# Joint attention and feed-forward on one core: last chunk's scores in quarters, a range check by bits and sums, last sums of x kept in SBUF, shape changes counted in the planner

## The chip, the cores and the metric

The kernel runs on one core of a Trainium2 chip. The time is the device time of one execution in microseconds. Five engines work side by side, each through its own queue in order: TensorE (PE in the profile, its weight loads PEld), VectorE (DVE), ScalarE (ACT), GpSimd (POOL) and SyncE (SP), which here issues every DMA.

## What is computed

Four batches of 12 heads, 448 positions, 64 values a head, everything in float32; then a feed-forward layer from 768 to 2048 and back.

```python
scores = scale * np.matmul(q, k.transpose(0, 1, 3, 2))     # q, k, v: (4, 12, 448, 64)
scores = cap * np.tanh(scores / cap)
scores = scores - np.max(scores, axis=-1, keepdims=True)
attn = np.exp(scores)
attn = attn / (np.sum(attn, axis=-1, keepdims=True) + 1e-09)
x = np.matmul(attn, v)             # then heads side by side: (1792, 768)
h = x @ w_in                       # w_in (768, 2048)
g = np.where(h >= 1, h, np.where(h <= -1, 0.0, (h + 1) ** 2 / 4.0))
out = (g @ w_out).astype(np.float32)
```

## The kernel before

**Numbers.** A float32 factor is split into a high and a low f16 half, and a product is three f16 matmuls (high by high, high by low, low by high). The weights arrive as 64-bit floats, read as pairs of 32-bit words, and are converted by bit operations (`piece`, L288 to L295, with a copy of the float32 in DRAM, zd). That fits weights in a bounded range only, so a second pass, `piece_check` (L305, L307), loads each of the 56 half pieces again into one of two buffers z0, z1 (32 halves of w_in with 384 elements a partition, 24 of w_out with 512) and takes their largest and smallest magnitude by two VectorE reductions. `piece_done` and `verdict` (L325 to L337) bring this and checks on x, g and the exponentials to one flag, with a reduction over the partitions on GpSimd (L330); at the end the flag is loaded (L1385) and a branch (L1386) skips a general program if all is in range.

**Attention.** Heads go in pairs n = 0 to 23, six to a batch. The 448 keys of a pair are chunks c = 0 to 3: three of 128 keys for each head, with two blocks of scores each, and a last one that holds the last 64 keys of both heads, with zeros in between. `qk` (L381) makes a chunk's scores in PSUM by three matmuls per block; for c < 3 they use 64 rows (L381, 64\*128) and the two heads' matmuls run in two halves of the array; for c = 3 they are full (128\*128). `expo` (L389, L391) takes tanh and exp on ScalarE into one of five buffers e. `av` multiplies with v. For the 18 pairs outside HALVED this is a float32 matmul (L458), half as wide for c < 3, full for c = 3; for n = 12 to 17 (HALVED) e and v are split into f16 first (L399, L400 into z0, z1 and eh0; L447). `norm` (L479) sums e over keys with four column tiles; for every second pair `divide` (L489) takes the reciprocal of both pairs, `spread` (L503) brings it to the rows of x, L506 multiplies and gives xf, which is split into f16 (L516, L354).

**Feed-forward.** Batches 0 and 1 are done plainly: `h_mm` (L573 to L575, 288 matmuls), the gate on ScalarE (L583, L584) and VectorE (L585), and `o_mm` (L609 to L611, 288). Batches 2 and 3 are done together by a scheme with seven products for eight (`product`, L758, 1008 matmuls), which needs sums of x over the two batches and the two halves of the columns, and the like of the weights (L773, L780, L781, from zd) and of g. For it xf of pairs 12 to 23 is stored to DRAM (xd, L508) and `pair_up` loads four of them (L733, into a ring xl of two tiles in eh0 and two in vh), and subtracts and adds (L735).

**What sets the order.** The steps are recorded with estimated costs, and a planner (`Plan`) lists them greedily for each engine in several rounds; the order of each engine's queue is fixed when the program is built. An engine's queue is in order, so what waits holds up what stands behind it; SP's queue as well.

Of the kernel before, what the change touches and what calls it, by code (L numbers as in the profile page):

```python
# [17 lines left out]
P = 128  # L18
# [4 lines left out]
VC = 2 * NCK  # L23
# [14 lines left out]
CX = 2 * NT  # L38
# [26 lines left out]
WINDOW, BWINDOW, ROUNDS = 25, 0, 10  # L65
# [4 lines left out]
KP = S + D  # L70
# [7 lines left out]
GROUP, HOLD = 4, 8000  # L78

# [4 lines left out]
class Plan:  # L84
# [4 lines left out]
    def __init__(self):  # L89
        self.steps, self.buffers, self.lead, self.held = [], {}, 0.0, False  # L90
# [23 lines left out]
    def run(self, before, after, prio, window, forward):  # L114
# [4 lines left out]
        free, open_, out, dma, grouped = {}, {}, [], 0.0, False  # L119
# [8 lines left out]
        while len(out) < n:  # L128
# [23 lines left out]
            if e == "PE":  # L152
                grouped = self.steps[i][4]
            end[i] = free[e] = t + cost
# [35 lines left out]
def fast_body(ctx, tc, flag, qkp, vp, cap, w_in, w_out, out):  # L190
# [19 lines left out]
    chk, chr_, chp = new("chk", [P, NCHK]), new("chr", [P, NCHK]), new("chp", [P, 2, NT, 2])  # L210
    w1 = new("w1", [P, 2, NFC, NCC, P], F16)
    w2 = ring("w2_", NEC, [P, 2048])
    raws = w2 + [new("raw", [P, 2048])]
    zs = ring("z", 2, [P, NFC * EH])
    qkr = ring("qkr", 2, [P, S + KP])
# [21 lines left out]
    xd = {n: dr.tile([P, S], F32, name="xd%d" % n) for n in range(PAIRED, B * NPR)}  # L237
# [23 lines left out]
    def pe(cost, fn, r, w):  # L261
        either(r, w, ("PE", cost, fn))
# [34 lines left out]
    def piece_check(i, part):  # L297

        k = i - NP1
        width = (NCC * P if k < 0 else NFC * EH) // 2  # L300
        zt, zk = take("z", zs)
        t = zt.bitcast(I32)[:, :2 * width]
        hi = t.rearrange("p (n two) -> p n two", two=2)[:, :, 1].bitcast(F32)
        src = (w_in[i] if k < 0 else w_out[k])[:, part * width:(part + 1) * width]
        dma(8 * P * width, lambda: M.dma_start(t, src.bitcast(I32)), [], zk)  # L305
        for j, op in ((0, ALU.max), (1, ALU.min)):
            dve(width, lambda j=j, op=op: V.tensor_reduce(out=chp[:, j, i, part:part + 1], in_=hi, op=op, axis=AX.X, apply_absolute_value=True), zk, [("chp", (j, i, part))])  # L307

    def piece_done():
        for j, op in ((0, ALU.max), (1, ALU.min)):  # L310
            dve(2 * NT, lambda j=j, op=op: V.tensor_reduce(out=chk[:, j * NT:(j + 1) * NT], in_=chp[:, j], op=op, axis=AX.X), [("chp", None)], [("chk", "p%d" % j)])
# [11 lines left out]
    def verdict():  # L323
# [4 lines left out]
        for a, z in ((NT, CX), (CS + ND, CF)):  # L328
            dve(z - a, lambda a=a, z=z: V.tensor_scalar(chk[:, a:z], chk[:, a:z], scalar1=-1.0, scalar2=None, op0=ALU.mult), [("chk", None)], [("chk", None)])
        pool(480, lambda: G.partition_all_reduce(chr_, chk, channels=P, reduce_op=bass_isa.ReduceOp.max), [("chk", None)], [("chr", None)])  # L330
        dve(NCHK, lambda: V.memset(okt, 1.0), [], [("rr0", None)])
        for a, z, lo, hi in ((0, NT, WMAX, WTOP), (NT, CX, -WTOP, -WMIN), (CX, CX + 2, 4.0, 61440.0), (CX + 2, CG, XS / 16.0, 2.0 * XS), (CG, CS, math.sqrt(GS) * S / 4, FTOP * S), (CS, CS + ND, 0.0, 1.0 / (S / 2)), (CS + ND, CF, -1.0, -1.0 / 61000.0), (CF, NCHK, -1.0, -1.0)):
            dve(NCHK, lambda a=a, z=z, lo=lo: V.tensor_scalar(okt[:, a:z], chr_[:1, a:z], scalar1=lo, scalar2=None, op0=ALU.is_ge), [("chr", None)], [("rr0", a)])
            dve(NCHK, lambda a=a, z=z, hi=hi: V.scalar_tensor_tensor(out=okt[:, a:z], in0=chr_[:1, a:z], scalar=hi, in1=okt[:, a:z], op0=ALU.is_le, op1=ALU.mult), [("chr", None), ("rr0", a)], [("rr0", a)])
# [33 lines left out]

    def qk(n, cs):
# [13 lines left out]
        pe(70 + 570 * len(cs), run, [(k, (z, i)) for z in parts for i in range(2)], [x for c in cs for x in st["s", n, c][1]])  # L383

    def expo(n, c):
# [3 lines left out]
        act(w * S + 60, lambda: A.activation(e[:, :w], s[:, :w, :S], AF.Tanh, scale=tsc), sk + [("tsc", None)], ek)  # L389
# [23 lines left out]
    def add(n, c):  # L413
# [9 lines left out]
        elif c == 3 < direct(n):  # L423
            t, tk = st["sums", n]
            for j in range(2):
                h = slice(j * D, (j + 1) * D)
                dve(S, lambda h=h, j=j: V.tensor_tensor(out=t[h, j], in0=t[h, j], in1=e[h, 0], op=ALU.add), ek + tk, tk)

    def last(v):

        return v[:, TC - 1:].rearrange("p c d -> p (c d)")

    def av(n, cs):
# [3 lines left out]
        if n in HALVED:  # L437
            vh, vk = st["vh", n]

            def run():  # L440
                for c in cs:
                    e = st["eh", n, c][0]
                    for x, y in ((0, 0), (0, 1), (1, 0)):
                        for j in range(2 if c < 3 else 1):
                            h = slice(j * D, (j + 1) * D)
                            o, w, m = (a[h, :S], vh[:, x, j * 3 + c], e[:, y, j]) if c < 3 else (a[:, :S], last(vh[:, x]), e[:, y, 0])
                            T.matmul(o, lhsT=w, rhs=m, start=(c == x == y == 0), stop=(c == 3 and x == 1))  # L447
            pe(105 + 570 * len(cs), run, [k for c in cs for k in st["eh", n, c][1]] + vk + (ak if cs[0] else []), ak)
# [3 lines left out]
        def run():  # L452
            for c in cs:
                e = st["e", n, c][0]
                for j in range(2 if c < 3 else 1):
                    h = slice(j * D, (j + 1) * D)
                    o, w, m = (a[h, :S], vt[:, j * 3 + c], e[:, j]) if c < 3 else (a[:, :S], last(vt), e[:, 0])
                    T.matmul(o, lhsT=w, rhs=m, start=(c == 0), stop=(c == 3))  # L458
        pe(105 + 800 * len(cs), run, [k for c in cs for k in st["e", n, c][1]] + vk + (ak if cs[0] else []), ak)
# [930 lines left out]
```

## Time and profile before

| | us |
|---|---|
| median of 3 runs | 629.85 |
| lowest, highest | 629.53, 630.63 |
| the profiled execution, its own time | 629.29 |
| its span in the trace | 627.4 |
| TensorE busy | 593.9 |
| VectorE busy | 518.4 |
| ScalarE busy | 424.2 |

The span lies within the execution's own time; 1.9 us lie around it. Busy times are sums of the intervals in which an engine has an instruction at work. A matmul's record is longer than the distance to the next one, since matmuls overlap; prices on TensorE are therefore taken from start to start.

### The profile page before, as it was taken

Reading aid. Unit: us, or ns where it says so; the run is one execution under the profiler, and the core shown is the slowest. Engines: PE = TensorE matmul, PEld = TensorE weight load, DVE = VectorE, ACT = ScalarE, POOL = GpSimd, SP = SyncE. Lnnn points to the kernel's source line nnn. Section 1 sums busy time; section 2 is a strip of 40 time slices with the busy share of each in tenths; the row PEclk is TensorE's granted clock in tenths of the full one; section 3 lists DMA queues with packets and bytes.
Section 4 is the critical chain, followed back from the end, with each engine's and each line's share of the span. In section 5 each row is a group of like instructions: output and inputs, shape, how many; then the busy total and the mean of one; then the engine's idle time right before and its main releaser. Section 6 shows DMA issues by size and latency. Waiting matters only on the chain.

```text
span 627.4 us, 9468 instructions
## 1 busy us (share of the span) xinstructions
PE 593.9 (95%) x3488; PEld 276.6 (44%) x3488; DVE 518.4 (83%) x929; ACT 424.2 (68%) x640; POOL 1.2 (0%) x6
## 2 busy tenths in 40 slices
PE   8989899999999899999999999988999989989995
PEld 2333454343454444444444444443444445534442
DVE  6996999999998557987847677799899989999654
ACT  7997977999863659999836459344888767452100
POOL 0000000000000000000000000000000000000000
PEclk9999999999999999999999999997999999999998
DMA  8894738375795311122166576685845667666672
GB/s 334 324 347 144 257 127 317 129 254 179 260 322 182 125 40 47 50 63 64 57 215 204 159 226 183 212 292 170 252 147 179 189 216 219 212 204 224 221 232 71
DMA packets 45130, 119.99 MB, mean 191 GB/s; under 512 B 5010, under 2 KB 19474, under 8 KB 43538
## 3 DMA queue, kind: packets, MB, share of 16 engines
q1 hardware_dynamic: 45072, 119.30, 57.1%
q8 instruction: 29, 0.48, 0.3%
q14 instruction: 27, 0.22, 0.1%
q10 hardware_dynamic: 2, 0.00, 0.0%
HBM read 91.10 MB, written 28.18 MB: 190 GB/s over the span
## 4 chain that ended last, share of the span: by engine, by line
PE 37%; DVE 27%; ACT 21%; DMA 7%; issue 6%; SPq 0%; POOL 0%; DVEq 0%; ACTq 0%; POOLq 0%
ACT e L389 5%; PE av L458 5%; PE s L381 4%; ACT e L391 4%; PE s L758 4%; PE f L573 3%; PE f L574 3%; PE f L575 3%; PE f L609 3%; PE f L611 3%; PE f L610 3%; DMA zd<-z 2%; ACT r L583 2%; DMA z<-w_out 2%; DVE z L291 2%
## 5 line engine op out<-in xcount | busy, mean ns | idle before, releaser
L758 PEld LDWEIGHTS <-w 128*128 128x128 f16 x720 | 70.6, 98 | 73.2 <-issue 8.6
L389 ACT ACTIVATE e<-s,tsc 128x896 f32<-128x896 f32 (+1 forms) x96 | 85.0, 905 | 15.4 <-PE s L381 12.5
L307 DVE TENSOR_REDUCE chp<-z 128x1 f32<-128x384 f32 (+1 forms) x112 | 63.6, 604 | 30.5 <-DMA z<-w_in 18.9
L573 PE MATMUL f<-x,w 128*128 128x448 f16 x192 | 67.8, 353 | 2.7 <-DVE wr L585 1.7
L381 PE MATMUL s<-spl 64*128 64x448 f16 (+1 forms) x504 | 67.0, 354 | 3.4 <-ACT e L389 3.4
L575 PE MATMUL f<-x,w 128*128 128x448 f16 x192 | 67.7, 352 | 0.3 <-DVE x L354 0.3
L391 ACT ACTIVATE e<-e,capb 128x896 f32<-128x896 f32 x72 | 67.0, 948 | 1.4
L609 PE MATMUL f<-g,w 128*128 128x448 f16 x192 | 67.8, 353 | 0.0
L611 PE MATMUL f<-g,w 128*128 128x448 f16 x192 | 67.7, 352 | 0.0
L610 PE MATMUL f<-g,w 128*128 128x448 f16 x192 | 67.7, 352 | 0.0
L574 PE MATMUL f<-x,w 128*128 128x448 f16 x192 | 67.7, 352 | 0.0
L458 PE MATMUL av<-e,vt 128*64 128x448 f32 (+1 forms) x252 | 65.0, 559 | 1.0 <-ACT e L391 1.0
L381 PEld LDWEIGHTS <-spl 64*128 64x128 f16 (+1 forms) x504 | 22.5, 95 | 48.0 <-issue 33.3
L419 DVE TENSOR_TENSOR sums<-e,e 128x896 f32<-128x896 f32 x24 | 26.1, 1089 | 14.9 <-ACT e L391 14.5
L584 ACT ACTIVATE r<-r 128x448 f32<-128x448 f32 x64 | 36.9, 576 | 1.5
L458 PEld LDWEIGHTS av<-e,vt 128*64 128x64 f32 (+1 forms) x252 | 18.0, 143 | 32.9 <-issue 24.3
L354 DVE SCALAR_TENSOR_TENSOR spl<-qkr,spl 128x960 f16<-128x960 f32 (+2 forms) x25 | 27.8, 1112 | 4.6 <-ACT spl L366 3.2
L295 DVE SCALAR_TENSOR_TENSOR w<-z,w 128x768 f16<-128x768 f32 (+1 forms) x28 | 29.9, 1068 | 2.0 <-ACT w L294 1.8
L294 ACT ACTIVATE w<-z 128x768 f16<-128x768 f32 (+1 forms) x24 | 22.7, 947 | 11.9 <-DVE z L291 11.8
L573 PEld LDWEIGHTS <-w 128*128 128x128 f16 x192 | 18.8, 98 | 20.8 <-issue 4.5
L574 PEld LDWEIGHTS <-w 128*128 128x128 f16 x192 | 18.8, 98 | 20.4 <-issue 4.5
L609 PEld LDWEIGHTS <-w 128*128 128x128 f16 x192 | 18.8, 98 | 19.8 <-issue 3.4
(256 smaller groups left out, 1076.6 us busy)
## 6 DMA issues: line engine op xcount, KB each, us to landing
z<-w_in SPq DMA_DIRECT2D x32, 384.0 KB, 3.2
z<-w_out SPq DMA_DIRECT2D x24, 512.0 KB, 4.6
qkr<-qkp SPq DMA_DIRECT2D x23, 480.0 KB, 3.6
w<-w_in SPq DMA_DIRECT2D x14, 768.0 KB, 7.1
w<-w_out SPq DMA_DIRECT2D x7, 1024.0 KB, 6.3
vt<-vp SPq DMA_DIRECT2D x24, 256.0 KB, 3.5
zd<-z SPq DMA_DIRECT2D x16, 384.0 KB, 2.9
zd<-z SPq DMA_DIRECT2D x12, 512.0 KB, 3.7
```

What stands on the lines that cost most here:

```text
L307: dve(width, lambda j=j, op=op: V.tensor_reduce(out=chp[:, j, i, part:part + 1], in_=hi, op=op, axis=AX.X, apply_absolute_value=True), zk, ...
L381: T.matmul(s[:, j, :S], lhsT=t[h, a, S + c * P:S + (c + 1) * P], rhs=t[h, b, :S], start=(i == 0), stop=(i == 2))
L389: act(w * S + 60, lambda: A.activation(e[:, :w], s[:, :w, :S], AF.Tanh, scale=tsc), sk + [("tsc", None)], ek)
L391: act(w * S + 110, lambda: A.activation(e[:, :w], e[:, :w], AF.Exp, scale=capb, **bias), ek + [("tsc", None)], ek)
L458: T.matmul(o, lhsT=w, rhs=m, start=(c == 0), stop=(c == 3))
L573: T.matmul(ph, lhsT=w1[:, 0, fc, c], rhs=x[c][0][:, 0], start=(c == 0), stop=False)
L574: T.matmul(ph, lhsT=w1[:, 1, fc, c], rhs=x[c][0][:, 0], start=False, stop=False)
L575: T.matmul(ph, lhsT=w1[:, 0, fc, c], rhs=x[c][0][:, 1], start=False, stop=(c == NCC - 1))
L609: T.matmul(po, lhsT=hi[:, fc], rhs=gv[:, 0], start=(fc == 0), stop=False)
L610: T.matmul(po, lhsT=lo[:, fc], rhs=gv[:, 0], start=False, stop=False)
L611: T.matmul(po, lhsT=hi[:, fc], rhs=gv[:, 1], start=False, stop=(fc == NFC - 1))
L758: T.matmul(t, lhsT=lhs(x, c), rhs=rhs[c][0][:, y], start=(first and c == i == 0), stop=(stop and c == n - 1 and i == 2), skip_group_check= ...
```

## The change

**Last chunk.** Its keys and values no longer carry zeros as padding for scores (KP 512 to 448). Scores come from twelve matmuls of 64 rows, 64 columns and 224 elements: two halves of the queries by two heads by three halves of f16; the four positions of the array are all used (own.start, other.start), two of the tiles write one bank of s, two the other. Tanh then reads 224 columns from each bank. The product with v is four matmuls 64 columns wide and 224 long (`last_av`), for which v comes with two more blocks (VC 8 to 10).

**Range check.** A half piece is loaded, its high words are masked and flipped in place by one VectorE step, and ScalarE takes a Relu with a sum over the elements, which is 0 if all are in range; per piece one reduction of 64 elements remains as a check from below. The half pieces from number 36 on use z1 alone, since z0 becomes part of the ring xl.

**Last sums of x.** xf of pairs 22 and 23 stays in SBUF; they are not stored, and `pair_up` uses them in place. The ring xl has two more tiles, in z0.

**Planner.** A step on TensorE has a kind, and 95 ns are added where the kind changes; some costs are others, and there are 20 rounds for 10. WS and XS are 2^12 for 2^13.

```diff
-WINDOW, BWINDOW, ROUNDS = 25, 0, 10
+WINDOW, BWINDOW, ROUNDS = 25, 0, 20
...
+CHANGE = 95.0
...
+                first, last = self.kinds.get(i, "ff")
+                cost += CHANGE * ((first if forward else last) != kind)
+                kind = last if forward else first
...
-        zt, zk = take("z", zs)
+        zt, zk = take("z", zs) if 2 * i + part < BOTH else (zs[1], [("z1", None)])
...
-        for j, op in ((0, ALU.max), (1, ALU.min)):
-            dve(width, lambda j=j, op=op: V.tensor_reduce(out=chp[:, j, i, part:part + 1], in_=hi, op=op, axis=AX.X, apply_absolute_value=True), zk, [("chp", (j, i, part))])
+        if part == 0:
+            dve(PEEK, lambda: V.tensor_reduce(out=chk[:, i:i + 1], in_=hi[:, :PEEK].bitcast(F32), op=ALU.max, axis=AX.X, apply_absolute_value=True), zk, [("chk", i)])
+        dve(width, lambda: V.tensor_scalar(hi, hi, scalar1=TOPS, scalar2=TOPV, op0=ALU.bitwise_and, op1=ALU.bitwise_xor), zk, zk, fast=True)
+        act(width + 250, lambda: A.activation(hi.bitcast(F32), hi.bitcast(F32), AF.Relu, accum_out=chp[:, i, part:part + 1]), zk, zk + [("chp", (i, part))])
...
+    def quarters():
+        part = lambda j: slice(j * D, (j + 1) * D)
+        return [(j, half, part(j), part((j + half) % 2), slice(half * HS, (half + 1) * HS)) for half in range(2) for j in range(2)]
+
+    def last_av(a, v, e, stop):
+        for j, half, own, other, cols in quarters():
+            T.matmul(a[own, cols], lhsT=v[:, VC - 4 + 2 * half + j], rhs=e[:, cols], start=False, stop=stop, skip_group_check=True)
...
-                    for j, h in enumerate([slice(j * D, (j + 1) * D) for j in range(2)] if c < 3 else [slice(0, P)]):
+                    if c == 3:
+                        for j, half, own, other, cols in quarters():
+                            T.matmul(s[other, half, :HS], lhsT=t[own, a, S + c * P:S + KP], rhs=t[own, b, cols], start=(i == 0), stop=(i == 2), tile_position=(own.start, other.start))
+                        continue
...
-            if n >= PAIRED:
+            if PAIRED <= n < B * NPR - 2:
                 dma(4 * P * S, lambda n=n, xf=xf: M.dma_start(xd[n], xf), fk, [("xd", n)])
...
-    xl = [eh0f[:, :S], eh0f[:, S:2 * S]] + [flat(t.bitcast(F32))[:, :S] for t in vhs]
+    xl = [eh0f[:, :S], eh0f[:, S:2 * S]] + [flat(t.bitcast(F32))[:, :S] for t in vhs] + [z0f[:, :S], z0f[:, S:2 * S]]
...
-        srcs = [(xd[n], ("xd", n)) for n in (PAIRED + k, 3 * NPR + k, 3 * NPR + HC + k, PAIRED + HC + k)]
+        srcs = [(xd[n], ("xd", n)) if n < B * NPR - 2 else st["xf", n] for n in (PAIRED + k, 3 * NPR + k, 3 * NPR + HC + k, PAIRED + HC + k)]
```

**The order.** Six pieces follow, of the kernel before and of the changed one. A row has the source line, the operation, and out<-in by tile names with the buffer's number; source lines of the changed kernel are higher by some 25 to 33.

ScalarE among the heads n = 12 to 17, before: exponentials (L391), f16 halves (L399, L516), and the gate of `h_mm` (L583, L584).

```order
L391 ACTIVATE e_101<-e_101,lnes,capb 128x896
L391 ACTIVATE e_97<-e_97,lnes,capb 128x896
L399 CAST z_90<-e_101 128x896
L516 ACTIVATE g_120<-wr_138 128x448
L583 ACTIVATE r_136<-f_142,half 128x448
L584 ACTIVATE r_136<-r_136 128x448
L516 ACTIVATE g_121<-wr_139 128x448
L583 ACTIVATE r_137<-f_143,half 128x448
L584 ACTIVATE r_137<-r_137 128x448
L516 ACTIVATE g_122<-wr_138 128x448
L389 ACTIVATE e_98<-s_140,tsc 128x896
L391 ACTIVATE e_98<-e_98,lnes,capb 128x896
```

Three gates stand within twelve rows. The same part of the program in the changed kernel, where L378 splits q and k, L415 and L417 are tanh and exp, L425 a half, L507 the copy of a head's product, L542 a half of g:

```order
L417 ACTIVATE e_95<-e_95,lnes,capb 128x896
L425 CAST z_87<-e_98 128x448
L378 ACTIVATE spl_91<-qkr_89 128x896
L415 ACTIVATE e_96<-s_138,tsc 128x896
L415 ACTIVATE e_97<-s_139,tsc 128x448
L425 CAST z_88<-e_99 128x896
L417 ACTIVATE e_96<-e_96,lnes,capb 128x896
L542 ACTIVATE g_129<-wr_136 128x448
L417 ACTIVATE e_97<-e_97,lnes,capb 128x448
L425 CAST eh_100<-e_95 128x896
L507 COPY xf_133<-av_142 128x448
L415 ACTIVATE e_98<-s_138,tsc 128x896
```

No gate of `h_mm` stands there: the heads have moved closer to each other on ScalarE, the gates to later rows.

SP's queue at the last stores and loads of xf before (L508 store, L733 loads, L812 loads of zd for sums of weights, L587 a store of g):

```order
L733 DMA vh_103<-xd_184 128x448
L812 DMA e_101<-zd_155 128x768
L812 DMA e_100<-zd_147 128x768
L508 DMA xd_185<-xf_135 128x448
L587 DMA gd_0_186<-vt_95 128x448
L733 DMA eh_102<-xd_176 128x448
L733 DMA eh_102<-xd_182 128x448
L733 DMA vh_103<-xd_185 128x448
L733 DMA vh_104<-xd_179 128x448
```

In the changed kernel there is no store or load of the last pair; L316 is the load of a check, L765 the loads of xd into z0, L845 loads of zd, L643 and L613 stores:

```order
L845 DMA e_99<-zd_154 128x768
L845 DMA e_98<-zd_146 128x768
L316 DMA z_87<-w_out 128x1024
L643 DMA out<-wr_137 128x448
L316 DMA z_88<-w_out 128x1024
L765 DMA z_87<-xd_173 128x448
L765 DMA z_87<-xd_179 128x448
```

The loads of pairs 13 and 19 have moved into z0 and stand behind checks, ahead of others.

VectorE's last rows before (L333, L334, L336 and L337 are of the verdict; L768 is the last sum of a product):

```order
L333 TENSOR_SCALAR rr_132<-chr 1x3
L333 TENSOR_SCALAR rr_132<-chr 1x1
L768 SCALAR_TENSOR_TENSOR wr_139<-av_144,wr_139 128x448
L334 SCALAR_TENSOR_TENSOR rr_132<-chr,rr_132 1x3
L334 SCALAR_TENSOR_TENSOR rr_132<-chr,rr_132 1x1
L336 TENSOR_REDUCE rr_132<-rr_132 1x1
L337 TENSOR_SCALAR fi<-rr_132,f 1x1
L1385 TENSOR_LOAD fi
```

And in the changed kernel, with L345 to L349 of the verdict and L801 the last sum:

```order
L345 TENSOR_SCALAR rr_130<-z_88 1x3 x2
L345 TENSOR_SCALAR rr_130<-z_88 1x1
L346 SCALAR_TENSOR_TENSOR rr_130<-z_88,rr_130 1x3 x2
L346 SCALAR_TENSOR_TENSOR rr_130<-z_88,rr_130 1x1
L348 TENSOR_REDUCE rr_130<-rr_130 1x1
L349 TENSOR_SCALAR fi<-rr_130,f 1x1
L801 SCALAR_TENSOR_TENSOR wr_137<-av_142,wr_137 128x448
L1417 TENSOR_LOAD fi
```

The verdict's last steps have moved ahead of the last sum.

## Rows read from the trace of the kernel before

**Rows 1.** The page, part 1: busy us of each engine, with share and instructions.
```profile
PE 593.9 (95%) x3488; PEld 276.6 (44%) x3488; DVE 518.4 (83%) x929; ACT 424.2 (68%) x640; POOL 1.2 (0%) x6
```

**Rows 2.** Busy time by stretch; columns: stretch, us, PE, PEld, DVE, ACT, POOL, PEclk, DMA share, GB/s.
```profile
10.00:50.00 40.00, 37.25 (x289) 13.23 (x293) 35.93 (x54) 38.72 (x48) 0.00 (x0) 1.00 0.91 336
...
229.60:309.00 79.40, 78.97 (x509) 37.36 (x506) 64.37 (x103) 77.11 (x117) 0.00 (x0) 1.00 0.17 51
309.00:395.00 86.00, 86.00 (x523) 38.72 (x522) 58.05 (x101) 52.48 (x70) 0.00 (x0) 1.00 0.62 190
...
420.00:440.00 20.00, 14.39 (x66) 6.73 (x65) 18.73 (x41) 9.54 (x17) 0.00 (x0) 0.83 0.62 185
440.00:560.00 120.00, 113.95 (x594) 57.72 (x592) 113.05 (x228) 87.31 (x161) 0.00 (x0) 1.00 0.64 204
560.00:580.00 20.00, 17.14 (x84) 8.30 (x83) 19.66 (x39) 7.02 (x13) 0.00 (x0) 0.91 0.63 208
```

**Rows 3.** Order of time, TensorE: start us, us, engine, line, operation, tiles, form, count.
```profile
334.07 1.42 PE L381 MATMUL s<-spl 64*128 64x448 f16 x9
335.41 1.72 PE L458 MATMUL av<-e,vt 128*64 128x448 f32 x8
337.07 0.36 PE L609 MATMUL f<-g,w 128*128 128x448 f16 x1
...
338.03 0.35 PE L611 MATMUL f<-g,w 128*128 128x448 f16 x1
338.31 1.31 PE L381 MATMUL s<-spl 64*128 64x448 f16 x12
339.55 0.48 PE L503 MATMUL t<-mix,sel 128*128 128x224 f32 x2
```

**Rows 4.** Order of time, TensorE, at a sum of exponentials by column tiles.
```profile
347.92 0.58 PE L479 MATMUL t<-sums,ones 128*32 128x224 f32 x8
348.32 0.56 PE L479 MATMUL t<-e,halves 128*32 128x224 f32 x8
```

**Rows 5.** Order of time, TensorE, at the last chunk of an f32 head.
```profile
107.63 1.92 PE L458 MATMUL av<-e,vt 128*64 128x448 f32 x6
109.49 0.74 PE L381 MATMUL s<-spl 64*128 64x448 f16 x6
```

**Rows 6.** Groups by line: out<-in, count, then busy us, mean ns, idle before.
```profile
L307 DVE TENSOR_REDUCE chp<-z 128x1 f32<-128x384 f32 (+1 forms) x112 | 63.6, 604 | 30.5 <-DMA z<-w_in 18.9
...
L584 ACT ACTIVATE r<-r 128x448 f32<-128x448 f32 x64 | 36.9, 576 | 1.5
...
L289 DVE TENSOR_SCALAR z<-w 128x768 int32<-128x768 int32 x14 | 7.7, 550 | 0.7 <-DMA w<-w_in 0.7
```

**Rows 7.** Order of time at the first product of sums of x, all engines.
```profile
416.50 0.61 DVE L506 SCALAR_TENSOR_TENSOR xf<-xf,t 128x448 f32<-128x448 f32 x1
...
417.14 0.32 SPq L508 DMA_DIRECT2D xd<-xf  x1
...
421.67 0.80 SPq L733 DMA_DIRECT2D vh<-xd  x2
...
426.64 1.41 PE L758 MATMUL s<-sums,qkr 128*128 128x448 f16 x3 [5.61 <-ACT sums L516]
```

**Rows 8.** DMA issues: out<-in, queue, operation, count, KB each, median us to landing.
```profile
z<-w_in SPq DMA_DIRECT2D x32, 384.0 KB, 3.2
z<-w_out SPq DMA_DIRECT2D x24, 512.0 KB, 4.6
```

**Rows 9.** Order of time at the wait of 2.36 us, all engines.
```profile
563.44 0.69 DVE L307 TENSOR_REDUCE chp<-z 128x1 f32<-128x512 f32 x1
563.59 0.63 PE L758 MATMUL f<-sums,w 128*128 128x448 f16 x2 [2.36 <-ACT sums L516]
```

**Rows 10.** Order of time at the end.
```profile
619.81 0.62 DVE L768 SCALAR_TENSOR_TENSOR wr<-av,wr 128x448 f32<-128x448 f32 x1 [1.41 <-PE av L758]
...
620.84 0.20 DVE L337 TENSOR_SCALAR fi<-rr,f 1x1 int32<-1x1 f32 x1
```

More of the change, by code (lines that the diff above doesn't have):

```diff
@@ L89, in __init__ @@
     def __init__(self):
-        self.steps, self.buffers, self.lead, self.held = [], {}, 0.0, False
+        self.steps, self.buffers, self.lead, self.held, self.kinds = [], {}, 0.0, False, {}
     def add(self, options, reads=(), writes=(), size=0):
@@ L209, in fast_body @@
     racc = new("racc", [P, B, 1])
-    chk, chr_, chp = new("chk", [P, NCHK]), new("chr", [P, NCHK]), new("chp", [P, 2, NT, 2])
+    chk = new("chk", [P, NCHK])
     w1 = new("w1", [P, 2, NFC, NCC, P], F16)
@@ L259, in pool, with pe @@
         either(r, w, ("Pool", cost, fn))
-    def pe(cost, fn, r, w):
+    def pe(cost, fn, r, w, kind="ff"):
+        plan.kinds[len(plan.steps)] = kind
         either(r, w, ("PE", cost, fn))
@@ L424, in add @@
             t, tk = st["sums", n]
[L425 to L431, printed above, removed]
+            tq, eq = t.rearrange("p j (h s) -> p (j h) s", h=2), e[:, 0].rearrange("p (h s) -> p h s", h=2)
+            for rows, at, of in ((slice(0, D), slice(0, 4, 3), slice(0, 2)), (slice(D, P), slice(2, 3), slice(0, 1)), (slice(D, P), slice(1, 2), slice(1, 2))):
+                dve(HS * len(range(2)[of]), lambda rows=rows, at=at, of=of: V.tensor_tensor(out=tq[rows, at], in0=tq[rows, at], in1=eq[rows, of], op=ALU.add), ek + tk, tk)
     def av(n, cs):
@@ L443, in run @@
                     for x, y in ((0, 0), (0, 1), (1, 0)):
-                        for j in range(2 if c < 3 else 1):
+                        if c == 3:
+                            last_av(a, vh[:, x], e[:, y, 0], x == 1)
+                            continue
+                        for j in range(2):
                             h = slice(j * D, (j + 1) * D)
-                            o, w, m = (a[h, :S], vh[:, x, j * 3 + c], e[:, y, j]) if c < 3 else (a[:, :S], last(vh[:, x]), e[:, y, 0])
-                            T.matmul(o, lhsT=w, rhs=m, start=(c == x == y == 0), stop=(c == 3 and x == 1))
-            pe(105 + 570 * len(cs), run, [k for c in cs for k in st["eh", n, c][1]] + vk + (ak if cs[0] else []), ak)
+                            T.matmul(a[h, :S], lhsT=vh[:, x, j * 3 + c], rhs=e[:, y, j], start=(c == x == y == 0), stop=(c == 2 and x == 1), skip_group_check=True)
+            pe(20 + 570 * len(cs), run, [k for c in cs for k in st["eh", n, c][1]] + vk + (ak if cs[0] else []), ak, "aa")
             return
@@ L454, in run @@
                 e = st["e", n, c][0]
-                for j in range(2 if c < 3 else 1):
+                if c == 3:
+                    last_av(a, vt, e[:, 0], True)
+                    continue
+                for j in range(2):
                     h = slice(j * D, (j + 1) * D)
-                    o, w, m = (a[h, :S], vt[:, j * 3 + c], e[:, j]) if c < 3 else (a[:, :S], last(vt), e[:, 0])
-                    T.matmul(o, lhsT=w, rhs=m, start=(c == 0), stop=(c == 3))
-        pe(105 + 800 * len(cs), run, [k for c in cs for k in st["e", n, c][1]] + vk + (ak if cs[0] else []), ak)
+                    T.matmul(a[h, :S], lhsT=vt[:, j * 3 + c], rhs=e[:, j], start=(c == 0), stop=(c == 2), skip_group_check=True)
+        pe(20 + 800 * len(cs), run, [k for c in cs for k in st["e", n, c][1]] + vk + (ak if cs[0] else []), ak, "aa")
     def sums_at():
@@ L477, in run @@
                     m = sm if c is None else st["e", n, c][0]
-                    w, m = (ones[:, g], m[:, j, half]) if c != 3 else (halves[:, g, j], m[:, 0, half])
+                    w, m = (ones[:, g], m[:, j, half]) if c != 3 else (halves[:, g, (j + (half.start > 0)) % 2], m[:, 0, half])
                     T.matmul(t[q:q + 32, :S // 2], lhsT=w, rhs=m, start=(g == 0 and c is None), stop=(g == 1 and c == (late[-1] if late else None)), tile_position=(0, q))
-        pe(500 + 400 * len(late), run, mk + [k for c in late for k in st["e", n, c][1]] + [("ones", None), ("halves", None)] + (tk if g else []), tk)
+        pe(450 + 375 * len(late), run, mk + [k for c in late for k in st["e", n, c][1]] + [("ones", None), ("halves", None)] + (tk if g else []), tk, "tt")
         act(S, lambda: A.copy(xf, a[:, :S]), ak, fk)
@@ L802, in keep_g @@
     def keep_g():
-        if turn["g17"] < NFC + 1:
+        if turn["g17"] < NFC:
             turn["g17"] += 1
```

63 lines of the change are left out of this document (37 added, 26 removed).

## The prediction

> **What bounds the kernel now.** I read the busy times first: TensorE is at work for 593.9 of 627.4 us [rows 1], so work taken from it should come back as time, unless it is taken where another engine is late. The second view is the busy time by stretch [rows 2]. From 309 to 395 us TensorE is busy all the time, and from 229.6 to 309 within 0.5 us of it; but there ScalarE is at 77.11 of 79.40, so two engines are full at once. From 10 to 50 us ScalarE (38.72 of 40) is ahead of TensorE (37.25): the first attention heads run with no feed-forward work beside them. From 420 to 440 TensorE has 14.39 of 20, with a mean granted clock of 0.83, so part of it at the lower level, 1.2 GHz; from 560 to 580 it has 17.14 at 0.91, and VectorE 19.66 of 20. The third view is the order of time around these two holes [rows 7, 9], which names the waits: 5.61 and 2.36 us, both for a ScalarE cast of a sum (of x, and of g). The last view is the run of matmuls [rows 3 to 5], from which I take every price on TensorE. Full 448-column f16 matmuls follow each other by 0.19 us (five steps from 337.07 to 338.03). Those on half the rows go in pairs at the price of one: twelve, two chunks, take from 338.31 to 339.55, which is 6 x 0.19 and 0.1 where the shape changes. A block with six of these and the three full ones of a last chunk takes 1.34 (334.07 to 335.41), 9 - 3 = 6 steps of 0.19 and twice 0.1.
>
> **Scores of the last chunk.** Before, three matmuls of 448 columns, 3 x 0.19 = 0.57 us for each of 24 head pairs; after, twelve on a quarter of the array, 224 columns each. No row shows quarters. The nearest are two: half-row tiles run in twos for the price of one [rows 3], and column tiles of 224 columns in fours, the eight matmuls of two passes in 0.40 us [rows 4]. By these, twelve quarters are three sets of 224 columns, 3 x 0.095 = 0.285 us. The bounds are 0.285 with four side by side, 0.57 with two, 12 x 0.095 = 1.14 with one. I take 0.285, to which both kinds of tiles point. Gain 24 x 0.285 = **6.8**. Places where a matmul's shape differs from the next one's are 191 before and 192 after, counted in both orders, so the planner's charge for them brings 0.
>
> A rule of the Trainium skill speaks against this part: PSUM — Partial Sum Buffer, section "PSUM bank collisions raise a hardware error ⚠️", quotes that "different row tiles are not able to access the same PSUM bank at the same time". The first two quarters are different row tiles that write one bank. The same section adds that writes collide within one bank and one quarter of the partitions, which these two don't share. Read strictly, the sum would be that of the first rival below; by the addition it stands, and no row here has two row tiles in one bank.
>
> **Values of the last chunk.** In the f32 heads a chunk of pairs and the last, full-width chunk take 1.86 us together (107.63 to 109.49 [rows 5]), two chunks of pairs 1.66 (335.41 to 337.07 [rows 3]); both streams have as many columns. Of the 0.20 a change of shape is 0.1, which is in the count above; the other 0.10 goes with the full width. 18 such heads: **1.8**, between 0 (the new half-length matmuls reload as often) and 3.6. The six halved heads keep their columns. TensorE's own work falls by 8.6.
>
> **Where that is not time.** (a) Pairs 2 to 5 run where ScalarE is ahead (10 to 50 us, [rows 2]), so that their share of the gain (4 x 0.38 = 1.5) is lost, and by the order ScalarE has 51 instructions between the copies of pairs 1 and 5 where it had 44; four of the seven are 896-wide and about 1 us each. TensorE gets 9 feed-forward matmuls there in return, 1.7 us, and some scores. I charge **2.3**. (b) The stretch from 229.6 to 309 runs from the reciprocal of pairs 12 and 13 to that of 16 and 17. By the order, 267 feed-forward matmuls stood between these points and 165 do now (the first two pieces of order show it: hardly a gate row is left between the exponentials). 102 x 0.19 = 19.4 less for TensorE, and 1.5 from the last chunks: 79.0 - 20.9 = 58. ScalarE loses 18 of 108 instructions, most 448 wide at 0.58 [rows 6]: 77.1 - 10 = 67. ScalarE becomes the limit, for some 9 us of TensorE's time; the displaced matmuls cost the same later on. If ScalarE works ahead in the stretch before, it is less: the floor is 0, the ceiling 10. I take **8**, near the ceiling, since five buffers of exponentials bound how far it can be ahead.
>
> **The last sums of x.** Before, xf of the last pair is multiplied at 416.50, stored at 417.14, loaded from 421.67 on, and the product starts at 426.64 [rows 7]: 10.1 us. After, it is neither stored nor loaded, and what is left (multiply, subtract, cast, the rest of the split) is four or five operations of about 0.6, 3 us. The order differs too: from the last norm to the first such product TensorE has 92 matmuls before and 166 after, 62 of them behind the spread of the last pair. 62 x 0.19 = 11.8 us cover the 3, so the wait goes. This stretch has lost 20.0 - 66 x 0.19 = **7.5** us, low clock included [rows 2]; that is the gain I take. Next late would be the loads of pairs 13 and 19, which now go into z0 behind its last check (third and fourth pieces of order); if they are, the gain falls towards 0. The ceiling is 8.
>
> **The range check.** The 112 reductions are 63.6 us of VectorE [rows 6], two to each of 56 half pieces. After, one and/xor pass: the nearest row is 550 ns at 768 strided elements [rows 6], so 0.3 to 0.45 at 384 to 512; and a Relu with a sum on ScalarE, about 0.6 by the 576 ns at 448 [rows 6]. VectorE gets back some 35 us, ScalarE pays nearly as much. ScalarE is far from full where the checks stand now. VectorE's relief is time only where it is full and TensorE waits: from 560 to 580, where a reduction of a check ends just before the cast's operand is worked on [rows 9]. There 20.0 - 84 x 0.19 = 4.0 us are lost; I take **2.5**, the wait of 2.36, between 4 and -3. The loss is possible because from piece 36 on the checks have z1 alone: SP's queue is in order, and a load that waits for a Relu holds up the loads and stores behind it. A load of 512 KB lands after 4.6 us [rows 8], so one turn is 5 to 6 us; the last nine loads start 343, 293, 247 to 49 matmuls from the end, 65 us for nine turns, which fits.
>
> **The end.** Before, four small VectorE operations stand behind the last sum and end at 621.04 [rows 10]; after, they stand ahead of it (the last two pieces of order). I take **0.7** of the 1.2 us, floor 0, as the last store must end anyway.
>
> **Sum.** 629.3 (the profiled execution) - 8.6 + 2.3 + 8 - 7.5 - 2.5 - 0.7 = 620.3. The median of the runs is 0.6 above that execution, hence **621.0**, 1.4% faster.
>
> **Rivals.** *Quarters in twos*, by the rule above, or because weights can't be loaded every 95 ns: a block costs 0.57 as before, 621 + 6.8 - 1.1 (pairs 2 to 5, where it costs nothing) = 626.7. For it: no set of tiles in the trace is shorter than 0.19 us. Against: fours of column tiles come at the price of one. 0.08. *Quarters one by one*: 24 x 0.855 = 20.5 more, 641.5, slower than before. It decides once a block costs over 0.57 + 8.3/24 = 0.92 us. Against it are both kinds of tiles in the rows; for it, that none had two row tiles write one bank. 0.04. *Checks hold ScalarE*: its queue is in order too, and 27 Relus now stand among the exponentials of pairs 18 to 23, each behind a load (3.2 us for 384 KB [rows 8]) and a VectorE pass. With two buffers in turn a pair of checks needs about 4.5 us; where they stand closer, exponentials wait, and TensorE for them. At 0.35 us each it is 9 us: 630. For it: pairs of Relus follow each other there with little between; against: ScalarE has but 52.48 of 86 us to do there now [rows 2], and the displaced matmuls are cover. 0.12. *The transition's wait stays*, behind z0's checks: 628.5. 0.05. *The change doesn't do what it says*: the new check finds the weights out of range and the general program runs, a multiple of the time. 0.01, as the new bounds take in normal weights of these sizes. My forecast has 0.70.
>
> **How the numbers follow.** Differences under 0.2%, 1.3 us, can't be told from no change here. The forecast's own range is 612 (ScalarE's stretch costs nothing) to 626. The twos, the wait that stays and most of the held ScalarE lie below 631; the range is 612 to 631 and leaves out serial quarters and sums of stalls. Slower by over 0.2%: 0.04 + 0.01, 0.04 of the held ScalarE, and 0.04 for several stalls at once, 0.13. Within 0.2%: the rest of the held ScalarE and half of the wait that stays, 0.11. Faster: 0.76.
>
> **What would show it.** Twelve quarters within 0.3 to 0.35 us (right), 0.57 or 1.1 (wrong). TensorE short by 5 to 10 us between the reciprocals of pairs 13 and 17, with ScalarE full. No wait for a cast behind the last norm, and a clock of 1.00 there. The last Relu ahead of the last matmul by some us. If exponentials stand behind loads of weights, the third rival holds; if SP's queue is late with sums' operands, the forecast is too low.

## The result and the profile after

The changed kernel takes 620.72 us, the median of runs from 618.24 to 622.51, against 629.94 for the kernel before beside it: a ratio of 0.985, 95% interval 0.9814 to 0.9886. The forecast was 621.0. A second set of runs gave 618.18 and a ratio of 0.9829 (0.9801 to 0.9857).

The profiled execution took 618.24 with a span of 616.4 us, 11.0 less than before. First the page's busy times of the changed kernel, to be read beside [rows 1]: TensorE has lost 9 us of busy time, VectorE 36, and ScalarE has gained 34.

```profile
PE 584.9 (95%) x3866; PEld 283.7 (46%) x3866; DVE 482.6 (78%) x903; ACT 458.1 (74%) x754; POOL 1.2 (0%) x6
```

Then busy time by stretch (columns as in [rows 2]). The second row runs from the reciprocal of pairs 12 and 13 to that of pairs 16 and 17.

```profile
10.00:50.00 40.00, 34.98 (x356) 14.09 (x352) 37.87 (x58) 39.31 (x51) 0.00 (x0) 1.00 0.92 343
223.20:287.90 64.70, 59.30 (x477) 29.37 (x473) 54.62 (x87) 64.31 (x94) 0.00 (x0) 0.97 0.23 68
300.00:380.00 80.00, 79.92 (x575) 37.83 (x574) 41.65 (x82) 61.45 (x113) 0.00 (x0) 1.00 0.54 164
412.00:440.00 28.00, 27.32 (x143) 13.88 (x142) 21.76 (x53) 20.08 (x43) 0.00 (x0) 1.00 0.53 165
440.00:550.00 110.00, 104.45 (x544) 52.87 (x543) 103.05 (x213) 85.30 (x163) 0.00 (x0) 1.00 0.74 231
550.00:570.00 20.00, 19.01 (x100) 9.50 (x99) 19.05 (x42) 10.63 (x21) 0.00 (x0) 1.00 0.75 229
```

ScalarE fills its stretch (64.31 of 64.70) and TensorE lacks 5.4 us there, where it lacked 0.4 before. Around the first product of the sums of x TensorE is busy for 27.32 of 28 us at a clock of 1.00 (14.39 of 20 at 0.83 before), and around 560 us, where there was a hole (17.14 of 20), it is busy for 19.01 of 20.

A last chunk in TensorE's order of time, beside [rows 3]:

```profile
335.49 0.74 PE L407 MATMUL s<-spl 64*128 64x448 f16 x6
336.16 0.48 PE L404 MATMUL s<-spl 64*64 64x224 f16 x12
336.58 1.72 PE L484 MATMUL av<-e,vt 128*64 128x448 f32 x8
```

Six half-row matmuls and the twelve quarters take 1.09 us (335.49 to 336.58), where six and three full ones took 1.34. The quarters themselves take 0.42 with the change of shape behind them: four side by side.

The transition and the end, both from the order of time of all engines (before: [rows 7, 10]):

```profile
410.29 0.54 PE L529 MATMUL t<-mix,sel 128*128 128x224 f32 x2
...
411.55 0.61 DVE L532 SCALAR_TENSOR_TENSOR xf<-xf,t 128x448 f32<-128x448 f32 x1
...
415.50 0.80 SPq L765 DMA_DIRECT2D z<-xd  x2
...
418.60 0.62 DVE L366 SCALAR_TENSOR_TENSOR sums<-vh,sums 128x448 f16<-128x448 f32 x1
...
420.92 1.17 ACT L542 CAST e<-z 128x448 f16<-128x448 f32 x2 [2.09 <-DVE chk L333]
...
422.14 1.02 PE L791 MATMUL s<-e,qkr 128*128 128x448 f16 x3 [0.51 <-ACT e L542]
...
423.00 0.73 PE L791 MATMUL s<-sums,qkr 128*128 128x448 f16 x3
...
607.36 0.20 DVE L349 TENSOR_SCALAR fi<-rr,f 1x1 int32<-1x1 f32 x1
...
609.83 0.62 DVE L801 SCALAR_TENSOR_TENSOR wr<-av,wr 128x448 f32<-128x448 f32 x1 [2.27 <-PE av L791]
```

The wait of 5.61 is one of 0.51, and it is for another operand: the sums with xf of pair 23, which `sums` holds, are split by 419.2, and TensorE waits for a cast of the sums in `e`, whose pairs 13 and 19 were loaded into z at 415.50. The flag is ready at 607.56, 2.3 us ahead of the last sum.

**Where the 11.0 us are.** From the first product of sums of x (`s<-sums,qkr`) on, both traces have 930 matmuls of the same form, so this point divides equal work. It starts 3.6 us earlier (426.64 to 423.00). From there to the start of the last matmul it was 192.8 us and is 186.4, 6.3 less; 929 x 0.189 = 175.6 of both is matmuls one behind the other, so what TensorE loses there fell from 17.2 to 10.9. From the start of the last matmul to the end of the span it was 8.0 and is 7.0.

### The profile page after: what moved, and what is told of

It is laid out like the page before. It is cut to its first block, busy times and chain, and to the rows that moved or that the text cites. A ratio compares the mean times of both kernels' runs of the same rounds, so it can differ in the third digit from the quotient of the medians.

```text
span 616.4 us, 10325 instructions
## 1 busy us (share of the span) xinstructions
PE 584.9 (95%) x3866; PEld 283.7 (46%) x3866; DVE 482.6 (78%) x903; ACT 458.1 (74%) x754; POOL 1.2 (0%) x6
## 4 chain that ended last, share of the span: by engine, by line
PE 30%; DVE 29%; ACT 25%; DMA 9%; issue 5%; SPq 0%; DVEq 0%; ACTq 0%
ACT e L415 6%; ACT e L417 6%; PE s L791 6%; DMA z<-w_out 4%; PE f L635 4%; PE f L636 3%; PE f L637 3%; DVE z L302 2%; PE av L484 2%; DVE z L301 2%; ACT r L609 2%; DMA gd<-vt 2%; PE s L407 2%; DVE w L306 2%; DVE g L545 2%
## 5 line engine op out<-in xcount | busy, mean ns | idle before, releaser
L791 PEld LDWEIGHTS <-w 128*128 128x128 f16 x720 | 70.1, 98 | 71.4 <-issue 4.3
L415 ACT ACTIVATE e<-s,tsc 128x896 f32<-128x896 f32 (+1 forms) x96 | 85.0, 905 | 5.1 <-DVE z L426 2.8
L417 ACT ACTIVATE e<-e,capb 128x896 f32<-128x896 f32 x72 | 67.2, 949 | 1.2
L320 ACT ACTIVATE z<-z 128x384 f32<-128x384 f32 (+1 forms) x56 | 34.0, 608 | 42.5 <-DVE z L319 41.5
L407 PE MATMUL s<-spl 64*128 64x448 f16 x432 | 49.7, 351 | 4.0 <-ACT e L415 3.8
L484 PE MATMUL av<-e,vt 128*64 128x448 f32 x216 | 48.1, 555 | 2.3 <-ACT e L417 1.9
L319 DVE TENSOR_SCALAR z<-z 128x384 int32<-128x384 int32 (+1 forms) x56 | 21.6, 388 | 23.1 <-DMA z<-w_out 15.2
L407 PEld LDWEIGHTS <-spl 64*128 64x128 f16 x432 | 17.9, 94 | 32.6 <-issue 20.8
L366 DVE SCALAR_TENSOR_TENSOR spl<-qkr,spl 128x896 f16<-128x896 f32 (+2 forms) x25 | 26.2, 1050 | 6.7 <-ACT spl L378 6.7
L599 PEld LDWEIGHTS <-w 128*128 128x128 f16 x192 | 18.8, 98 | 22.0 <-issue 6.2
L542 ACT ACTIVATE g<-wr 128x448 f16<-128x448 f32 x37 | 21.0, 571 | 10.3 <-DVE wr L611 10.3
L635 PEld LDWEIGHTS <-w 128*128 128x128 f16 x192 | 18.7, 98 | 20.0 <-issue 3.9
```

The lines of the kernel that those rows point to most:

```text
L415: act(w * S + 60, lambda: A.activation(e[:, :w] if c < 3 else e[:, 0].rearrange("p (h s) -> p h s", h=2), s[:, :w, :S] if c < 3 else s[:, ...
L417: act(w * S + 110, lambda: A.activation(e[:, :w], e[:, :w], AF.Exp, scale=capb, **bias), ek + [("tsc", None)], ek)
L484: T.matmul(a[h, :S], lhsT=vt[:, j * 3 + c], rhs=e[:, j], start=(c == 0), stop=(c == 2), skip_group_check=True)
L599: T.matmul(ph, lhsT=w1[:, 0, fc, c], rhs=x[c][0][:, 0], start=(c == 0), stop=False)
L635: T.matmul(po, lhsT=hi[:, fc], rhs=gv[:, 0], start=(fc == 0), stop=False)
L791: T.matmul(t, lhsT=lhs(x, c), rhs=rhs[c][0][:, y], start=(first and c == i == 0), stop=(stop and c == n - 1 and i == 2), skip_group_check= ...
```

## What the experiments showed

Except where it is said, these kernels keep the order of every queue of the kernel that they start from. The changed kernel again, quarters twice, xf stored and the and/xor pass three times ran side by side. In the later sets only the kernel before ran beside them; its medians differ by 0.4 us between all sets, and the changed kernel's 618.18 is the measure there too.

**The changed kernel again**, as the measure for the others.

> The changed kernel unchanged, beside which the next three are read. All theories: 620.7 us, within 1.5 us, as its own runs spread from 618.2 to 622.5.

Measured 618.18 (616.5 to 621.72), 2.5 below the first set and so outside the 1.5 that was allowed.

**Quarters twice.**

```diff
-                for i, (a, b) in enumerate(((0, 0), (0, 1), (1, 0))):
+                for i, (a, b) in enumerate(((0, 0), (0, 1), (1, 0)) * (2 if c == 3 else 1)):
+                    i = i % 3
```

> The changed kernel with the twelve quarter matmuls of every last chunk issued twice, the order on all engines otherwise the same. A block takes 0.31 us in the trace, so TensorE gets 24 x 0.30 = 7.2 us more, about what the quarters have saved. Theory: TensorE is the limit except among the first six pairs and in pairs 14 to 17, where ScalarE is; 14 to 18 of 24 blocks count, 4 to 5.5 us, so 625 to 626. Rival one, the saving of matmuls had no part in the gain and the order made it: under 1.5 us. Rival two, every block counts: 7.2 us.

Measured 619.82 (ratio 0.9855, 0.9827 to 0.9883), 1.6 more than the changed kernel. The work was really added, as TensorE's order of time shows:

```profile
336.29 0.77 PE L405 MATMUL s<-spl 64*64 64x224 f16 x24
336.99 1.72 PE L485 MATMUL av<-e,vt 128*64 128x448 f32 x8
```

0.70 us a block for 0.42. But the last reciprocal of attention comes at 391.2 where it came at 390.1: of 24 x 0.28 = 6.7 us only 1.1 arrive there. Matched matmul by matmul with the changed kernel beside it, what is added up to 300 us is all taken back, at waits of 0.2 to 2.1 us that TensorE has there for ScalarE or VectorE; what the last five blocks add from 308 to 380 us, 1.3, stays in full. By size the first rival nearly holds (1.6 for its 1.5; the two intervals leave some 2.5 us either way). In the new order TensorE's time in the last chunks is not on the path before 300 us, and it is on it behind.

**The full matmuls of the kernel before twice.** The same edit in the kernel before, whose last chunk has three full matmuls.

> The kernel before with the three full matmuls of every last chunk issued twice, its order otherwise the same: 24 x 0.57 = 13.7 us more on TensorE. In the changed kernel 7.2 us more in these places cost 1.6. Theory one: before, TensorE was the limit from 80 to 420 us, so 9 to 12 us more, and it is the new order that took this away. Theory two: TensorE's small gaps there take it up as they do after: 0 to 4 us more.

Measured 638.07 against 629.91 (ratio 1.013, 1.0108 to 1.0152), 8.2 us of 13.7; between the two theories, nearer to the first. Matched matmul by matmul with the trace of before, the lag grows by 0.57 at nearly every block after 100 us and keeps it, but for 1.5 us between 178 and 240; the seven blocks before leave 0.6 of 4.0. So before the change a microsecond of TensorE in these places was worth 0.6, and after it some 0.2. The saving was real under the old order; in the changed kernel another limit stands there up to 300 us. Whether its order or its Relus on ScalarE put it there, these two runs don't separate.

**xf of the last two pairs stored and loaded back.**

```diff
...
+                    also(scaled_at, lambda n=n, xf=xf: M.dma_start(xd[n], xf))
+                    also(len(plan.steps) - 1, lambda n=n, xf=xf: M.dma_start(xf, xd[n]))
```

(`also` appends to a step's instructions; n = 22, 23; the first behind the scaling, the second behind the split of x.)

> The changed kernel with xf of pairs 22 and 23 stored and loaded back into the same tile before the last sums, the order on all engines otherwise the same. Theory of the prediction (the store and load were the cause, but 62 matmuls, 11.8 us, now also cover them): the chain of 10 to 11 us just fits, 0 to 1.5 us more. Rival, keeping xf in SBUF is what removed the wait: 5 to 7.5 us more, with a wait for a cast of sums in front of the first such product.

Measured 626.13 (ratio 0.9941, 0.992 to 0.9961), 7.9 more: the rival. Its order of time at the place:

```profile
413.41 0.61 DVE L532 SCALAR_TENSOR_TENSOR xf<-xf,t 128x448 f32<-128x448 f32 x1
...
414.05 0.32 SPq L540 DMA_DIRECT2D xd<-xf  x1
...
418.98 0.32 SPq L541 DMA_DIRECT2D xf<-xd  x1
...
421.50 0.62 DVE L778 TENSOR_TENSOR xf<-xf,eh 128x448 f32<-128x448 f32 x1 [5.47 <-DMA xf<-xd]
...
429.94 0.73 PE L801 MATMUL s<-sums,qkr 128*128 128x448 f16 x3
```

VectorE stands still for 5.47 us until the load has landed, and the product starts at 429.94 for 423.26 beside it. So in this order the missing store and load are the cause: it would not have hidden them. Whether another order would is seen below (the last chunk alone).

**The and/xor pass three times.** `tensor_scalar` on the high words is issued three times in place of once.

> The changed kernel with the and/xor pass of each half piece issued three times, which leaves the same bits, so that a half piece costs VectorE about the 1.2 us of the two reductions before; the order is otherwise the same. 56 x 0.78 = 43.5 us more on VectorE. Theory: VectorE's relief is time only in the last third, where VectorE is full and TensorE waits: 2 to 4 us more. Rival one, VectorE's share never counted: under 1 us. Rival two, the one buffer z1 holds up the loads behind it as soon as a turn is 0.8 us longer: over 6 us more.

Measured 641.4 (ratio 1.0184, 1.0156 to 1.0212), 23 more than the changed kernel: by size the second rival, by a wide margin. ScalarE's longest list of waits (total us, times, longest), in the changed kernel and in this one:

```profile
ACT z L320 <- DVE z L319: 41.5, 25, 8.3
```

```profile
ACT z L320 <- DVE z L319: 65.7, 37, 6.7
```

The waits of the Relus for VectorE have grown from 41.5 to 65.7 us; but of the 41.5, 21.9 stand behind 560 us, where ScalarE has little else to do, so the sum is no price. A half piece is a loop: load, VectorE, Relu, and only then the next load into that buffer. Matched matmul by matmul with the changed kernel beside it, the lag is 5.2 us at 390 us, 12.1 at 440 and 23.3 at the end. From 300 to 390 us VectorE has room (60.83 of 90 us busy), and the Relus wait for 20.9 us where they waited for 11.7: there what is added to a turn is paid by ScalarE's queue and by what stands behind the Relu. Behind 440 us, where half of the 23 us arise, VectorE is nearly full (111.88 of 120 to 560), so the theory's own mechanism, at a higher price than it had, can do the same. How much is the loop and how much a full VectorE was not separated.

**Tanh twice.** Two of the four tanh of pairs 14 to 17 are issued twice, in another kernel those of pairs 19 to 22.

```diff
...
+            for _ in range(2 if n in range(14, 18) and c < 2 else 1):
+                A.activation(...)
...
```

> The changed kernel (618.2 us beside the last three runs) with the tanh of two of four chunks of pairs 14 to 17 issued twice, 8 x 1.0 us more on ScalarE there, the order otherwise the same. Theory: ScalarE is the limit of this stretch: 5 to 8 us more. Rival, TensorE is, and its idle time there comes from elsewhere: under 1.5 us.

> The same 8 us of ScalarE in pairs 19 to 22, where ScalarE is busy for 61 of 80 us and TensorE for 79.9. Theory: a control, 0 to 2 us more. Rival, suggested by the doubled quarters, whose 7 us cost 1.6: exponentials set the pace through the whole of attention: 5 to 8 us more.

Measured 626.99 (ratio 0.9957, 0.9938 to 0.9975) and 627.73 (0.9982, 0.996 to 1.0004): 8.8 and 9.5 more than the 618.18 of the set before (the kernel before is at 629.55 here, 629.81 there). In the traces, matched with the changed kernel of the set before, the first gets 6.0 us later between 223 and 288 us: as the theory has it, ScalarE limits pairs 14 to 17. The second is 7.4 us later at 390. It is not the control that it was meant to be: ScalarE has no room from 300 to 380 us either, although its busy share there is 61.45 of 80. Beyond that, the first loses 3.4 and the second 4.2 us between 440 and 460, at one wait and by the clock behind it, which is close to the lower of its two levels, 1.2 GHz. Here are the second's matmul with its wait (1.67 in the changed kernel), and five us of the second and of the changed kernel again:

```profile
456.24 2.40 PE L794 MATMUL s<-raw,w 128*128 128x448 f16 x6 [2.94 <-DVE vt L614]
```

```profile
455.00:460.00 5.00, 3.76 (x11) 1.54 (x11) 4.32 (x9) 4.70 (x10) 0.00 (x0) 0.54 0.89 212
```

```profile
455.00:460.00 5.00, 5.00 (x28) 2.57 (x27) 5.00 (x10) 5.00 (x10) 0.00 (x0) 1.00 0.87 258
```

What ScalarE's other 18.5 us from 300 to 380 are in the changed kernel, its order of time and its waits (total us, times, longest) say:

```profile
340.45 0.56 ACT L320 ACTIVATE z<-z 128x384 f32<-128x384 f32 x1
...
341.78 0.56 ACT L320 ACTIVATE z<-z 128x384 f32<-128x384 f32 x1 [0.69 <-DVE z L319]
...
344.94 0.55 ACT L320 ACTIVATE z<-z 128x384 f32<-128x384 f32 x1 [2.51 <-DVE z L319]
...
347.38 0.58 ACT L320 ACTIVATE z<-z 128x384 f32<-128x384 f32 x1 [1.80 <-DVE z L319]
...
349.02 1.90 ACT L415 ACTIVATE e<-s,tsc 128x896 f32<-128x896 f32 x2
```

```profile
ACT z L320 <- DVE z L319: 13.1, 8, 3.3
```

Three of these four Relus wait, 5.0 us in all, for VectorE's pass, with a tanh behind them in the queue; 13.1 of the 18.5 us are such waits. That is the third rival's mechanism, so the next two runs took the checks away.

**No checks.** The loads, and/xor passes, Relus and small reductions of the range check are left out, and constants stand for their results; then the same with the tanh of pairs 19 to 22 twice.

```diff
...
-        dma(8 * P * width, lambda: M.dma_start(t, src.bitcast(I32)), [], zk)
+        dma(8 * P * width, lambda: None, [], zk)
...
```

> The changed kernel without the range check's loads, and/xor passes, Relus and small reductions (small constants are written in their place), the order of all the rest the same. Theory one: the Relus that wait in ScalarE's queue for a load hold up exponentials and casts behind them, and a turn of the one buffer z1 holds up others; 3 to 7 us less than the changed kernel's 618 to 620.7. Theory two: the order leaves room for them and the checks cost nothing: 0 to 1.5 us less.

> The kernel before this one (no checks) with the tanh of two of four chunks of pairs 19 to 22 issued twice, 8 us more of ScalarE, which cost 9 us with the checks in place. Theory one: ScalarE's room there is used up by Relus that wait; without them 0 to 3 us more than without checks. Theory two: the exponentials set the pace by themselves: 6 to 9 us more.

Measured 613.5 (ratio 0.9738, 0.9713 to 0.9763) and 615.38 (0.9779, 0.9755 to 0.9803). Without checks the kernel gains 4.7 to 7.2 us, and the tanh that cost 9.5 beside the checks cost 1.9 without them: by size theory one, in both. Busy time by stretch without checks:

```profile
300.00:380.00 80.00, 80.00 (x575) 37.99 (x574) 31.70 (x83) 49.46 (x71) 0.00 (x0) 1.00 0.18 60
412.00:440.00 28.00, 28.00 (x151) 14.64 (x149) 19.97 (x52) 15.89 (x32) 0.00 (x0) 1.00 0.27 89
440.00:550.00 110.00, 107.22 (x563) 54.88 (x562) 103.86 (x222) 82.06 (x151) 0.00 (x0) 1.00 0.60 197
```

From 300 to 380 TensorE gains nothing by it (80.00 for 79.92): there the order had left the Relus just as much room as they take, and theory one's held-up exponentials cost nothing. The gain is behind 412, 151 matmuls for 143 and 563 for 544; whether the load, VectorE's pass or the Relu costs it there was not separated.

**The last chunk alone**, in the kernel before, listed anew by its planner.

> The kernel before with the last chunk alone changed (quarters for scores, four half-length matmuls for v, their costs in the planner; two small tiles of the check share other tiles for room); check, sums of x and planner are those of before, and the planner lists it anew. Theory one: TensorE's 8.6 us are worth 4 to 7 us: 623 to 626. Theory two: ScalarE's pace takes them up: 628 to 631.

Measured 622.3 (ratio 0.9877, 0.9855 to 0.9899), 7.6 less, more than theory one had. It can't be read as the price of the quarters, since the order changed with them:

```profile
239.60:297.90 58.30, 50.70 (x417) 24.07 (x413) 48.18 (x80) 56.91 (x79) 0.00 (x0) 0.94 0.23 73
...
420.00:440.00 20.00, 18.40 (x96) 9.21 (x95) 19.41 (x43) 9.46 (x18) 0.00 (x0) 1.00 0.64 202
```

ScalarE limits the same pairs here too (TensorE 50.70 of 58.30), and the hole at 420 us is all but closed (18.40 of 20 with 96 matmuls, 14.39 with 66 before) with store and load still in place. Its first product of sums of x waits for 0.49 us, and the second hole has closed as well, with both reductions of the check of before:

```profile
427.97 0.54 PE L776 MATMUL s<-sums,qkr 128*128 128x448 f16 x2 [0.49 <-ACT sums L533]
```

```profile
548.00:568.00 20.00, 19.24 (x101) 9.55 (x100) 20.00 (x42) 10.04 (x18) 0.00 (x0) 1.00 0.69 226
```

From this product to the start of the last matmul are 187.1 us, against 192.8 before and 186.4 in the changed kernel. The work there is that of before and only its order is new, so an order can close both holes without the kept xf and without the new check, and all that the change has beyond this kernel is worth 1.6 to 4.1 us. What an order alone brings stays open: the kernel before was not listed anew with nothing else changed.

**Other orders.** The planner holds back attention steps until four are ready or 8000 ns have passed; these two kernels have 4000 ns, and two steps, and are listed anew.

```diff
-GROUP, HOLD = 4, 8000
+GROUP, HOLD = 4, 4000
```

> The changed kernel with the planner's time for holding back grouped attention steps at 4000 for 8000, so with another order: between the norms of pairs 13 and 17 stand 204 feed-forward matmuls where the changed kernel has 165 (before: 267), and ScalarE has 85 instructions there for 90. Theory: the packing of pairs 14 to 17 costs 7 us of TensorE's time, and half or more of it comes back: 612 to 616. Rival, the idle time moves to another place: 617 to 620.

> The changed kernel with attention steps grouped from two on for four, again another order with less idle time of TensorE in the planner's own list. Theory as for the run before, with a little less: 613 to 617. Rival: 617 to 621.

Measured 611.65 (ratio 0.9721, 0.9698 to 0.9745) and 619.68 (0.9834, 0.9809 to 0.9858). The first beats both kernels. Its row for the stretch between the two reciprocals:

```profile
219.10:286.90 67.80, 65.35 (x515) 32.58 (x512) 57.44 (x96) 64.69 (x98) 0.00 (x0) 1.00 0.21 70
```

ScalarE's work is the same (64.69 for 64.31), but TensorE does 515 matmuls beside it where it did 477, and lacks 2.5 us for 5.4; its first product of sums of x starts at 417.69 for 423.00. The second kernel gave nothing; its idle time went elsewhere, as the rival has it. One of its six executions took 1529.92 us; the trace is of another one, and the cause is open (a flag out of range and the general program behind it would be one).

## Why the forecast was right, and which steps were not

By total, sign and range it held (621.0 for 620.72; in part by luck, see the end of this section). By its own steps:

- *Four quarters side by side*: right. A block is 0.25 us shorter, 6.0 us in all for 6.8; the first set of four takes 0.120 where 0.095 was assumed. By the strict sentence of the Trainium skill (PSUM — Partial Sum Buffer, "PSUM bank collisions raise a hardware error ⚠️") the two row tiles could not write one bank at the same time, 0.57 a block by the first rival. The trace, 0.42 with the change of shape behind it, goes with the same section's addition on quarters of the partitions.
- *The values, 1.8*: right. A chunk of pairs and the last one take 1.66 us where they took 1.76 or 1.86, by what followed.
- *Attention, -8.6 + 2.3 + 8 = 1.7 later*: right as a sum. The first product of sums starts 3.6 us earlier although a wait of 5.6 ahead of it has become one of 0.5, so attention and what else stands up to there is 1.5 later. ScalarE is the limit between the two reciprocals, as forecast, but TensorE lacks 5.0 us more there, for the 8 charged; the reciprocal of pairs 4 and 5 is 2.8 later, for the 2.3. As terms that could be added or undone one by one they were wrong: with ScalarE as the limit, the quarters are worth 1.6 us and not the 5.7 that the first rival's price rested on (quarters twice), and ScalarE's lack of room doesn't end with pair 17 (tanh twice in pairs 19 to 22). The view that misled was ScalarE's busy share among the pairs behind 17, 61.45 of 80 us in the changed kernel: most of the rest is waits that hold its queue. TensorE's share did not mislead: at 79.92 of 80 added matmuls arrive in full, and where they don't it has waits that show.
- *The wait at the last sums of x, -7.5*: right in size, and in this order in cause. 5.1 us of waiting are gone, and 2.7 of the 3.4 that TensorE lost in the first 20 us behind it, where the clock had been low: 7.8; putting store and load back cost 7.9. But it is no price of the store and load alone, since the kernel with the last chunk alone has them and waits for 0.49. The working of the cover was too short: multiply, subtract, cast and split were put at 3 us and take 7.6 (411.55 to 419.2), since VectorE's queue has other operations between them; 62 matmuls, 11.8 us, cover that too, with 4 to spare for the 8.8 by the working. What comes last is what the forecast had named as next late, the sums with pairs 13 and 19, loaded behind z0's last check: 0.51.
- *The range check, -2.5*: the time came at the place named, but not shown to be for the reason given. The stretch at 560 us lost 4.1 us by [rows 2], and loses 20.0 - 100 x 0.189 = 1.1 now; with the last chunk alone, and VectorE's reductions as before, it loses as little. The step that failed is that ScalarE, "far from full where the checks stand now", pays nothing in time: tanh beside the checks arrives in full, three passes for one cost 23 us, and no checks gain 4.7 to 7.2. Prices of single operations were well met, by the groups of the changed kernel:

```profile
L320 ACT ACTIVATE z<-z 128x384 f32<-128x384 f32 x32 | 17.8, 556 | 14.0 <-DVE z L319 13.1 <-DVE rr L343 0.9
...
L319 DVE TENSOR_SCALAR z<-z 128x384 int32<-128x384 int32 x32 | 11.5, 361 | 7.8 <-DMA z<-w_in 7.3
```

  361 ns on VectorE and 556 on ScalarE (0.3 to 0.45, and about 0.6, were forecast); a read of the accumulator of 190 ns behind each Relu was not. What was missing is the idle time in the same rows: these Relus hold ScalarE's queue for 14.0 us beside the 17.8 that they work.
- *The third rival*, checks that hold ScalarE: its mechanism is there, its time is not. It had 0.12; from 300 to 380 us taking the checks out gains nothing, so the order left the waits just enough room.
- *The end, -0.7*: 1.0. The working misread its row: 0.6 of the "1.2 us" is the last sum itself, which stays, so the four small operations had 0.6 to give. Where the other 0.4 comes from is open.

That the sum lies within 0.3 us of the median is luck. In the profiled execution 11.0 us are gone for the 9.0 forecast: attention, the transition and the end are each within 0.3 us of their terms, and the late part gained 3.6 for 2.5. But that execution is the fastest of its four, 2.5 below their median where 0.6 was allowed; the second set's median is 2.8 below the forecast.

## What to carry to other kernels

A busy share well under one doesn't mean that an engine has room: double a small piece of its work in an otherwise fixed order, match the two traces instruction by instruction, and see where it arrives. Here 8 us arrived as 7.4 at their place on a ScalarE with 77%; matmuls added to TensorE arrived in full where it had 99.9% and not at all where it had waits of its own. In a queue in order, an instruction that waits for a load takes up that engine for as long as it waits. A hole that closes along with a change is not yet closed by it: here a new order closed two of them with the old store, load and check in place. When a change saves work on one engine and a planner orders anew, look first at which engine the new order packs: another setting of the planner took 6 to 9 us off the changed kernel.

## What the runs showed of the hardware

Four matmul tiles of 64 rows, 64 columns and 224 elements run side by side, their starts 3 to 4 ns apart. They go two to a bank, on different rows and different columns of the array, and the two write different halves of the partitions of that bank: twelve in 0.42 us with the change of shape, twenty-four in 0.70. In the stretch where TensorE waits for ScalarE the mean granted clock fell from 1.00 to 0.97, and to 0.94 in the kernel with the last chunk alone. What a low clock adds to a wait shows in the second run with tanh twice: a wait longer by 1.3 us, with a granted clock of 0.54 in the five us around the matmuls behind it, made the kernel 4.2 us later.
